# Zero-padding a 64-row matmul to 128 rows, one more weight block kept on chip, and loads and queries moved behind a weight conversion

## The chip, the cores and the metric

The kernel runs on one NeuronCore of a Trainium2 chip. The metric is the device time of one execution in microseconds (us). Nearly all executions of one kernel here agree within 0.3%. A ratio is the mean time of one kernel's fast runs over that of the other kernel's fast runs of the same rounds, so it is not quite the ratio of the medians that stand beside it. "Faster" or "slower" is said for a difference clear of 2%.

Words used throughout: PE is TensorE's matmul pipeline, DVE is VectorE, ACT is ScalarE, POOL is GpSimd, SP is the engine that queues most transfers. In the timelines each of them starts its instructions in the order in which the kernel gives them (weight loads apart), and "in order" below means that. kvd is a unit's k'v as ScalarE copies it out, qT a transposed query, x_n a normalized query, g what follows from h (`maximum(h, 0)**2`), T1 the first difference of w_out's blocks, which product 5 needs. A matmul of 32-bit floats counts as two passes in the timelines (x8 is four matmuls), a transpose as one.

## The reference

```python
# attention without softmax: 8 batches, 8 heads, 576 tokens, head size 64
kv  = einsum('bhsd,bhse->bhde', k, v)                # k'v, contracted over the tokens
out = einsum('bhsd,bhde->bhse', q, kv)
x   = out / sqrt(mean(out*out, -1) + 1e-6) * g_norm  # then reshaped to 4608 x 512
# feed-forward: w_in 512 x 2048, w_out 2048 x 512, both given in 64-bit floats
h = x @ w_in
y = maximum(h, 0)**2 @ w_out
```

576 tokens are four chunks of 128 and a rest of 64. That rest is what the padding is about.

## The kernel before

The feed-forward part runs on nine strips of 512 tokens. Each big product is done by a scheme of seven smaller products on blocks and sums of blocks of the weights (numbers 1 to 7 in the code, taken in the order 1, 2, 6, 5, 7, 3, 4). The first strip's up products use the blocks directly, as the sums are not ready. The weights arrive as 64-bit floats and are turned into 32-bit ones on chip, 32 pieces in 16 pairs, by ScalarE and VectorE. w_out's sums go out to DRAM (`w_out`) and are fetched back block by block in every strip. All this happens while the first strip runs.

```python
def load_rest(b, eng):                       # the last 64 tokens: two batches share 128 partitions
    half = slice(REST * (b % 2), REST * (b % 2 + 1))
    ...
        eng.dma_start(out=rest[n, b // 2][half], in_=src[b, :, C * P : S].rearrange("h s d -> s h d"))

def convert_pieces(ids, dests):
    for i in range(acted[0], min(ids[-1] + 3, len(sources))):
        convert_on_act(i)                    # two ScalarE steps: they wait for the raw piece's load
        acted[0] = i + 1
    # ... four VectorE steps for each of the two pieces ...
    for _ in ids:
        load_piece()                         # next raw piece, into one of four buffers

def sums_out(j):
    t = [wt_pool.tile([P, 5, DH], FP32, name="wt", tag="wt") for _ in js]
    # ... four sums for each of two pieces ...
        nc.sync.dma_start(out=w_out[2:7, :, j, :].rearrange("b p e -> p b e"), in_=x)

def key_value(b, p):                         # one "unit": a batch and a pair of heads
    for c in range(C):
        nc.tensor.matmul(ps, lhsT=flat(tk[:, c]), rhs=tv[:, :, c, :], start=(c == 0), stop=False)
    nc.tensor.matmul(
        ps, lhsT=flat(rest["k", b // 2][half, 2 * p : 2 * p + 2]),      # 64 rows
        rhs=rest["v", b // 2][half, 2 * p : 2 * p + 2], start=False, stop=True,
    )
    # ... ScalarE copies to kvd ...
    if b > 0:
        load_next()                          # the next unit's k, v and q
```

The start, before the first up product:

```python
load_rest(0, nc.gpsimd)
load_piece()
for i in range(3):
    load_piece()
    load_next(nc.gpsimd)
...
for i in range(ready[0]):                    # attention of batch 0, one slice a step
    convert(i // 4 + 1)
    attend(i + 1)
```

## Time and profile before

| | before |
|---|---|
| median, range of the first runs | 1051.1 us, 1050.1 to 1052.0 |
| span of the profiled run, mean granted clock | 1049.1 us, 0.987 |
| PE, DVE, ACT busy | 96%, 40%, 25% |
| DMA moved | 126.6 MB |
| first up product starts | 52.4 us |
| product 6 of strip 0 starts (first to need a block back from DRAM) | 150.5 us |

How to read it: PE is full but for the first 150 us. The lines that show this stand in the prediction, which cuts the run at product 6 of strip 0.

### The profile page before, as it was taken

The page shows a single profiled execution, that of the slowest core. Times are in us where ns is not written, and L with a number is a line of the kernel's source. Part 1 is how long each engine was busy: PE and PEld are TensorE (multiplying, and loading weights), DVE is VectorE, ACT ScalarE, POOL GpSimd, SP SyncE. Part 2 cuts the span into 40 slices and gives each one's busy share as a digit, 9 for nine tenths or more (in the row PEclk, how much of TensorE's full clock was granted, in tenths as well). Part 3 has the DMA queues.
Part 4 walks back from the last instruction along what each step waited for, and adds up shares of the span by engine and source line. Part 5 has one row for each costly group of instructions (what it writes and reads, how often), then busy time and mean ns, then how long its engine had stood idle before and what let it go on. Part 6 is the DMA issues. An engine that isn't in the chain of part 4 may idle for free.

```text
span 1049.1 us, 12212 instructions
## 1 busy us (share of the span) xinstructions
PE 1002.4 (96%) x4864; PEld 855.6 (82%) x4864; DVE 424.3 (40%) x769; ACT 263.4 (25%) x546; POOL 18.4 (2%) x81
## 2 busy tenths in 40 slices
PE   3499799999999999999999999999999999999998
PEld 2444388888888888888888888888888888888887
DVE  2768774335323433333243425322433235413420
ACT  3668420221123211221132103210331122102200
POOL 4000000000000000000000000000000000000000
PEclk9699899999999999999999999999999999999999
DMA  9489965224433344136412650255112330242031
GB/s 239 137 222 303 314 214 178 83 61 128 139 106 85 86 134 147 31 87 189 152 31 61 176 165 26 57 164 186 50 31 91 131 101 1 90 145 87 1 131 70
DMA packets 119210, 126.63 MB, mean 121 GB/s; under 512 B 78225, under 2 KB 102801, under 8 KB 111345
## 3 DMA queue, kind: packets, MB, share of 16 engines
q1 hardware_dynamic: 118464, 124.41, 39.2%
q0 software_dynamic: 528, 1.44, 0.6%
q8 instruction: 38, 0.62, 0.3%
q14 instruction: 20, 0.16, 0.0%
q10 hardware_dynamic: 160, 0.00, 0.0%
HBM read 109.05 MB, written 16.78 MB: 120 GB/s over the span
## 4 chain that ended last, share of the span: by engine, by line
PE 88%; DMA 5%; DVE 3%; ACT 2%; issue 1%; SPq 0%; DVEq 0%; ACTq 0%
PE ps_A L390 45%; PE ps_B L390 22%; PE ps_C L390 11%; PE x_ps L300 2%; DMA raw<-in_moe_w_in_dram 2%; PE kv_ps L268 2%; DMA w_out<-wt 2%; PE xt_ps L327 2%; PE t_ps L253 1%; DMA raw<-in_moe_w_out_dram 1%; PE kv_ps L269 1%; PE ps_A L424 1%; ACT w_c L152 1%; DVE wt L186 1%; ACT raw L155 0%
## 5 line engine op out<-in xcount | busy, mean ns | idle before, releaser
L390 PE MATMUL ps_A<-w_blk,gt 128*128 128x256 f32 x1120 | 249.9, 379 | 0.0
L390 PEld LDWEIGHTS ps_A<-w_blk,gt 128*128 128x128 f32 x1120 | 211.2, 190 | 28.3 <-PE x_ps L295 0.2
L390 PE MATMUL ps_A<-x_t,w_in 128*128 128x256 f32 x768 | 182.4, 380 | 0.6 <-DVE gt L450 0.6
L390 PEld LDWEIGHTS ps_A<-x_t,w_in 128*128 128x128 f32 x768 | 143.8, 190 | 20.4 <-DVE gt L450 1.0
L390 PE MATMUL ps_B<-w_blk,gt 128*128 128x256 f32 x576 | 128.5, 379 | 0.0
L390 PEld LDWEIGHTS ps_B<-w_blk,gt 128*128 128x128 f32 x576 | 108.4, 190 | 14.4 <-issue 0.2
L186 DVE TENSOR_TENSOR gt<-gt 128x512 f32<-128x512 f32 (+1 forms) x54 | 66.2, 1226 | 72.1 <-PE ps_A L390 37.6
L400 ACT COPY snap<-ps_A 128x512 f32<-128x512 f32 x82 | 48.0, 585 | 169.8 <-PE ps_A L390 169.8
L450 DVE TENSOR_TENSOR gt<-ps_C,snap 128x512 f32<-128x512 f32 x32 | 22.1, 691 | 151.6 <-PE ps_C L390 151.6
L451 DVE SCALAR_TENSOR_TENSOR gt<-gt 128x512 f32<-128x512 f32 x96 | 66.4, 692 | 3.3
L450 DVE TENSOR_TENSOR gt<-ps_A,snap 128x512 f32<-128x512 f32 x32 | 22.1, 691 | 109.6 <-PE ps_A L390 109.3
L390 PE MATMUL ps_B<-xT,w_in 128*128 128x256 f32 x256 | 61.1, 382 | 0.0
L390 PE MATMUL ps_A<-xT,w_in 128*128 128x256 f32 x256 | 60.9, 381 | 0.0
L390 PE MATMUL ps_B<-x_t,w_in 128*128 128x256 f32 x256 | 60.5, 379 | 0.0
L390 PE MATMUL ps_C<-xT,w_in 128*128 128x256 f32 x256 | 60.5, 379 | 0.0
L390 PE MATMUL ps_C<-w_blk,gt 128*128 128x256 f32 x256 | 58.1, 381 | 0.0
L305 DVE TENSOR_REDUCE ms<-sq 128x8 f32<-128x512 f32 x36 | 24.6, 684 | 77.8 <-ACT sq L303 77.7
L390 PEld LDWEIGHTS ps_C<-xT,w_in 128*128 128x128 f32 x256 | 48.6, 190 | 6.6
L390 PEld LDWEIGHTS ps_A<-xT,w_in 128*128 128x128 f32 x256 | 48.2, 190 | 6.8
L390 PEld LDWEIGHTS ps_C<-w_blk,gt 128*128 128x128 f32 x256 | 47.7, 190 | 6.6 <-issue 0.2
L390 PEld LDWEIGHTS ps_B<-xT,w_in 128*128 128x128 f32 x256 | 47.6, 190 | 6.7
L390 PEld LDWEIGHTS ps_B<-x_t,w_in 128*128 128x128 f32 x256 | 47.6, 190 | 5.9
(78 smaller groups left out, 853.4 us busy)
## 6 DMA issues: line engine op xcount, KB each, us to landing
w_blk<-w_out SPq DMA_DIRECT2D x61, 1024.0 KB, 5.0
raw<-in_moe_w_in_dram SPq DMA_DIRECT2D x16, 512.0 KB, 5.2
k<-in_k_dram SPq DMA_DIRECT2D x64, 128.0 KB, 3.5
v<-in_v_dram SPq DMA_DIRECT2D x32, 256.0 KB, 3.7
raw<-in_moe_w_out_dram SPq DMA_DIRECT2D x16, 512.0 KB, 5.2
out_dram<-o_sb SPq DMA_DIRECT2D x64, 128.0 KB, 4.8
q<-in_q_dram SPq DMA_DIRECT2D x56, 128.0 KB, 3.5
w_out<-wt SPq DMA_DIRECT2D x8, 640.0 KB, 7.8
```

What stands on the lines that cost most here:

```text
L152: nc.scalar.activation(c, high_f, AF.Abs)
L186: eng.tensor_tensor(out=out, in0=a, in1=b, op=ALU.subtract)
L253: nc.tensor.transpose(ps[:, c, :], flat(t[:, c]), ident)
L268: nc.tensor.matmul(ps, lhsT=flat(tk[:, c]), rhs=tv[:, :, c, :], start=(c == 0), stop=False)
L269: nc.tensor.matmul(ps, lhsT=flat(rest["k", b // 2][half, 2 * p : 2 * p + 2]), rhs=rest["v", b // 2][half, 2 * p : 2 * p + 2], start=False, ...
L300: nc.tensor.matmul(o, lhsT=qT[b, p][:, c_b, :], rhs=kvd[b, p], start=True, stop=True)
L305: nc.vector.reduce_sum(out=ms, in_=by_head(sq), axis=AX.X)
L327: nc.tensor.transpose(ps[:, p, :], t[:, ts(p, P)], ident)
L390: nc.tensor.matmul(bank[BANK[p]][:, i, :], lhsT=lhsT(k), rhs=rhs(k), start=p in (1, 5, 2) and i == 0 and k == 0, stop=k == n - 1, skip_gro ...
L400: nc.scalar.copy(snap[p], b)
L450: nc.vector.tensor_tensor(out=o, in0=b, in1=a, op=ALU.add)
L451: nc.vector.scalar_tensor_tensor(out=o, in0=o, scalar=0.0, in1=o, op0=ALU.max, op1=ALU.mult)
```

## The change

Its intent: take the odd 64-row matmul out of PE's full part, and clear the stretch of the conversion of transfers and of work that can wait. Cut to its core:

```diff
+    k_rest = const.tile([P, H, D], FP32, name="k_rest")
+    v_rest = const.tile([P, 2, H, D], FP32, name="v_rest")     # zero outside batch b % 2's half
...
         nc.tensor.matmul(
-            ps, lhsT=flat(rest["k", b // 2][half, 2 * p : 2 * p + 2]),
-            rhs=rest["v", b // 2][half, 2 * p : 2 * p + 2], start=False, stop=True,
+            ps, lhsT=flat(k_rest[:, 2 * p : 2 * p + 2]), rhs=v_rest[:, b % 2, 2 * p : 2 * p + 2],
+            start=False, stop=True,
         )
...
-        if j + 2 == FQ:                                         # two blocks' stores, early
-            nc.sync.dma_start(out=w_out[0], in_=w_out_11)
-            nc.sync.dma_start(out=w_out[1], in_=w_out_21)
...
-        t = [wt_pool.tile([P, 5, DH], ...
+        t = [wt_pool.tile([P, 4, DH], ...                       # T1 goes to a spare slot of w_in
...
+                for b, t in enumerate(w_first):                 # three blocks' stores, late
+                    nc.sync.dma_start(out=w_out[b], in_=t)
...
-    load_rest(0, nc.gpsimd)
-    load_piece()
-    for i in range(3):
-        load_piece()
+    nc.gpsimd.memset(k_rest, 0.0)
+    nc.gpsimd.memset(v_rest, 0.0)
+    load_next(nc.gpsimd)
+    load_rest(0, nc.gpsimd)
+    for i in range(2):
         load_next(nc.gpsimd)
+        load_piece()
+        load_piece()
...
-        if b > 0:
+        if b < 2:
+            if p == 0:
+                load_next(nc.sync if b else nc.gpsimd)
+        else:
             load_next()
...
     for i in range(ready[0]):
-        convert(i // 4 + 1)
         attend(i + 1)
+        convert((i + 1) // 4)
...
+            if i in (n_up + 6, n_up + 7):                       # batch 2's loads
+                load_next()
+            if i == n_up + 8:
+                load_next()
+                load_rest(2, nc.sync)
...
+            if i < n_up:                                        # batch 1's units, then its queries
+                attend(ready[0] + max(0, (i + 1) - n_up + 2 * NP))
             else:
-                part = (i + 1 - n_up / 2) / (4 + n_up / 2)
-                attend(ready[0] + int((goal - 1 - ready[0]) * min(max(part, 0), 1)) + (part > 1))
+                attend(n_kv + (goal - n_kv) * min(i + 1 - n_up, 6) // 6)
```

The padding leaves the result as it was: `k_rest` holds the 64 rows of both batches of a pair, and the zeros in `v_rest` stand against the other batch's rows.

The parts hang together by memory. The padded `v_rest` takes twice the room of the old one, 4 KB a partition (2 x 8 x 64 x 4 bytes), and beside the old five-block results (4 buffers of 5 KB) the padded kernel did not fit when built alone. Keeping T1 in a slot of `w_in` that is free at that time makes a result 4 KB and so pays for the padding.

More of the change, by code (lines that the diff above doesn't have):

```diff
@@ L86 @@
     ctx.enter_context(tc.manual_schedule())
-    main, rest = {}, {}
+    main = {}
     def load(b, p, q_eng):
@@ L103, in load @@
             main[n, b, p] = t
+    k_rest = const.tile([P, H, D], FP32, name="k_rest")
+    v_rest = const.tile([P, 2, H, D], FP32, name="v_rest")
+    q_rest = {}
     def load_rest(b, eng):
-        half = slice(REST * (b % 2), REST * (b % 2 + 1))
-        for n, src in (("k", k), ("v", v), ("q", q)):
-            if b % 2 == 0:
-                rest[n, b // 2] = rest_pool.tile([P, H, D], FP32, name=f"{n}_rest", tag=f"{n}_rest")
-            eng.dma_start(out=rest[n, b // 2][half], in_=src[b, :, C * P : S].rearrange("h s d -> s h d"))
+        h = b % 2
+        half = slice(REST * h, REST * (h + 1))
+        if h == 0:
+            q_rest[b // 2] = rest_pool.tile([P, H, D], FP32, name="q_rest", tag="q_rest")
+        for t, src in ((k_rest[half], k), (v_rest[half, h], v), (q_rest[b // 2][half], q)):
+            eng.dma_start(out=t, in_=src[b, :, C * P : S].rearrange("h s d -> s h d"))
     units = [(b, p) for b in range(B) for p in range(NP)]
@@ L128 @@
     w_out = dram.tile([7, P, FQ, DH], FP32, name="w_out")
-    w_out_11, w_out_21 = (w_in[:, :, :, b].rearrange("p k g e -> p (k g) e") for b in (4, 5))
+    w_out_11, w_out_21, w_out_t1 = w_first = [
+        w_in[:, :, :, b].rearrange("p k g e -> p (k g) e") for b in (4, 5, 6)
+    ]
     w_in_v = moe_w_in.rearrange("(kc p) (b g f) -> kc g p b f", p=P, b=2, g=NG)
@@ L202, in pieces_out @@
         convert_pieces((NG * NP + j, NG * NP + j + 1), [dest(j), dest(j + 1)])
-        if j + 2 == FQ:
-            nc.sync.dma_start(out=w_out[0], in_=w_out_11)
-            nc.sync.dma_start(out=w_out[1], in_=w_out_21)
     def sums_out(j):
         js = (j, j + 1)
-        t = [wt_pool.tile([P, 5, DH], FP32, name="wt", tag="wt") for _ in js]
+        t = [wt_pool.tile([P, 4, DH], FP32, name="wt", tag="wt") for _ in js]
         convert_pieces([NG * NP + FQ + j for j in js], [x[:, 0:2, :] for x in t])
         for x, j in zip(t, js):
-            minus(nc.vector, x[:, 2], x[:, 0], w_out_11[:, j, :])
-        for x in t:
-            minus(nc.vector, x[:, 3], x[:, 1], x[:, 2])
+            minus(nc.vector, w_out_t1[:, j, :], x[:, 0], w_out_11[:, j, :])
+        for x, j in zip(t, js):
+            minus(nc.vector, x[:, 2], x[:, 1], w_out_t1[:, j, :])
         for x in t:
@@ L217, in sums_out @@
         for x, j in zip(t, js):
-            minus(nc.vector, x[:, 4], w_out_21[:, j, :], x[:, 3])
-            nc.sync.dma_start(out=w_out[2:7, :, j, :].rearrange("b p e -> p b e"), in_=x)
+            minus(nc.vector, x[:, 3], w_out_21[:, j, :], x[:, 2])
+            nc.sync.dma_start(out=w_out[3:7, :, j, :].rearrange("b p e -> p b e"), in_=x)
     conversions = [(pieces_in, i) for i in range(0, NG * NP, 2)]
@@ L229, in convert @@
             converted[0] += 1
+    nc.gpsimd.memset(k_rest, 0.0)
+    nc.gpsimd.memset(v_rest, 0.0)
+    load_next(nc.gpsimd)
     load_rest(0, nc.gpsimd)
-    load_piece()
-    for i in range(3):
+    for i in range(2):
+        load_next(nc.gpsimd)
         load_piece()
-        load_next(nc.gpsimd)
+        load_piece()
     g_col = const.tile([P, 1], FP32, name="g_col")
@@ L256, in transposed_query @@
         if b % 2:
-            t = rest["q", b // 2][:, 2 * p : 2 * p + 2]
+            t = q_rest[b // 2][:, 2 * p : 2 * p + 2]
             ps = apsum.tile([P, P], FP32, name="tr_ps", tag="at")
@@ L264, in key_value @@
         tk, tv = main.pop(("k", b, p)), main.pop(("v", b, p))
-        half = slice(REST * (b % 2), REST * (b % 2 + 1))
         ps = apsum.tile([P, P], FP32, name="kv_ps", tag="at")
@@ L283, in key_value @@
                 load_rest(b + 1, nc.sync)
-        elif p == 0:
-            load_next(nc.gpsimd)
     def query(n):
@@ L377 @@
     A_IN = {1: 0, 2: 2, 3: 6, 4: 3, 5: 4, 6: 5, 7: 1}
-    B_OUT = {1: 0, 2: 1, 3: 3, 4: 6, 5: 4, 6: 5, 7: 2}
+    B_OUT = {1: 0, 2: 1, 5: 2, 7: 3, 3: 4, 6: 5, 4: 6}
     bank, snap, gq, w_blk = {}, {}, {}, {}
@@ L460, in up @@
         combine(p, relu_squared(11), relu_squared(12), last, relu_squared(22))
-    to_stream = iter([(s, p) for s in range(N_STRIP) for p in ORDER][2:])
-    w_blk[0, 1], w_blk[0, 2] = w_out_11, w_out_21
+    w_blk[0, 1], w_blk[0, 2], w_blk[0, 5] = w_first
+    to_stream = iter([(s, p) for s in range(N_STRIP) for p in ORDER if (s, p) not in w_blk])
     def stream():
@@ L479, in down @@
         del w_blk[s, p]
-        if s > 0 or p not in (1, 2):
+        if s > 0 or p not in (1, 2, 5):
             stream()
@@ L529 @@
                     stream()
+                for b, t in enumerate(w_first):
+                    nc.sync.dma_start(out=w_out[b], in_=t)
             fn(*a)
-            if s == 0 and i == n_up:
-                sums_g(quarters(0, NG - 1))
-            if s == 0 and i == n_up + 6:
-                for g in range(NG):
-                    sums_in(g)
             done += w
@@ L538 @@
                 attend(ready[s] + int((goal - ready[s]) * min(done / (0.85 * total), 1)))
-            else:
-                part = (i + 1 - n_up / 2) / (4 + n_up / 2)
-                attend(ready[0] + int((goal - 1 - ready[0]) * min(max(part, 0), 1)) + (part > 1))
+                continue
+            if i == n_up:
+                sums_g(quarters(0, NG - 1))
+            if i in (n_up + 6, n_up + 7):
[3 more added lines that the diff above has]
+                load_rest(2, nc.sync)
+                for g in range(NG):
+                    sums_in(g)
+            n_kv = ready[0] + 2 * NP
+            if i < n_up:
+                attend(ready[0] + max(0, (i + 1) - n_up + 2 * NP))
+            else:
+                attend(n_kv + (goal - n_kv) * min(i + 1 - n_up, 6) // 6)
 _INS = ['q', 'k', 'v', 'g_norm', 'moe_w_in', 'moe_w_out']
```

## The prediction

> **What bounds the kernel now.** I read the page's top and slices first, then windows cut at the events of PE's timeline, then the waits of the stretch in which PE idles, then the chain of waits and the timelines that explain them.
>
> ```profile
> PE   3499799999999999999999999999999999999998
> PEclk9699899999999999999999999999999999999999
> DMA  9489965224433344136412650255112330242031
> ```
>
> A slice is 26 us. Only the first five slices are not full of PE, and there the DMA row is at 9. The windows give it in us (stretch, length, busy of PE, weight load, VectorE, ScalarE, GpSimd, clock, DMA share, GB/s):
>
> ```profile
> 0.00:13.90 13.90, 0.00 (x0) 0.02 (x1) 3.98 (x8) 3.74 (x5) 7.61 (x17) 1.00 0.87 177
> 13.90:30.60 16.70, 12.14 (x56) 10.15 (x56) 6.59 (x15) 8.11 (x18) 4.10 (x18) 0.90 1.07 286
> 30.60:52.40 21.80, 8.84 (x50) 7.63 (x49) 15.76 (x44) 11.96 (x24) 0.00 (x0) 0.68 0.37 119
> 52.40:100.00 47.60, 47.56 (x130) 22.82 (x130) 36.03 (x76) 36.13 (x81) 0.00 (x0) 0.97 0.89 254
> 100.00:132.70 32.70, 22.13 (x86) 12.16 (x87) 25.33 (x62) 17.50 (x47) 1.16 (x8) 0.90 1.08 317
> 132.70:150.50 17.80, 17.80 (x102) 16.05 (x101) 11.14 (x25) 4.40 (x10) 0.60 (x5) 1.00 0.81 276
> 150.50:1049.00 898.50, 893.88 (x4446) 786.79 (x4444) 325.46 (x544) 181.52 (x364) 4.91 (x34) 1.00 0.32 100
> ```
>
> 150.5 us is my checkpoint: there PE begins product 6 of strip 0's second matmul, the first that needs a w_out block which went to DRAM and came back. Behind it PE is full (only the last store, 4.6 us, is idle), so that part, 898.5 us, shrinks only if PE has less to do. Ahead of it are two bounds: a start of 52.4 us, and 100 to 132.7, in which PE idles 10.6 us while DMA is at 1.08. The waits of 60 to 150 us:
>
> ```profile
> ACT w_c L152 <- DMA raw<-in_moe_w_out_dram: 15.6, 5, 5.4
> PE x_ps L295 <- ACT kvd L278: 6.6, 1, 6.6
> SPq L469 <- DMA w_out<-wt: 6.0, 1, 6.0
> ```
>
> PE's longest wait is for kvd, but ScalarE was not slow: in its in-order queue that copy stood behind a conversion step waiting for its raw weight. The chain shows the same queue of transfers:
>
> ```profile
> 105.51 8.76 DMA w_out<-wt
> 115.56 9.09 DMA w_out<-wt
> ...
> 125.50 2.68 DVE wt L186 x8
> ```
>
> So what ends last ahead of the checkpoint is the conversion: its final pair of pieces leaves VectorE at 128.2 us, the last results are queued at 132.9 (behind batch 2's loads in the same queue), and the first blocks are asked back at 141.3.
>
> In the full part the extra work is one form:
>
> ```profile
> 201.49 1.05 PE L268 MATMUL kv_ps<-v,k 128*128 128x128 f32 x8
> 202.47 0.49 PE L269 MATMUL kv_ps<-v_rest,k_rest 64*128 64x128 f32 x2
> 202.89 1.99 PE L390 MATMUL ps_A<-x_t,w_in 128*128 128x256 f32 x8
> 204.72 1.89 PE L390 MATMUL ps_B<-x_t,w_in 128*128 128x256 f32 x8
> ```
>
> Read starts, not durations. Eight 128-row passes take 0.98 us to the next start, the two 64-row passes 0.42, and the eight passes behind them 1.83, where the same eight take 1.73 elsewhere.
>
> **What the Trainium skill says.** "TensorEngine Tiling (Array Packing)", Key Properties: changing the tiling mode drains TensorE, changing only the tile does not. The trace agrees: the passes on either side of the 64-row form are late. "TensorE: Matmul & The Clock Gate", LDWEIGHTS: the load's time follows the columns, not the rows contracted. Padding to 128 rows should then cost nothing; the trace has one column count only (186 ns for 64 rows, 192 for 128), which fits. Same page, Part 1: an idle window brings PE's clock down to half. The trace shows 0.68 in 30.6 to 52.4 us, and the first up product after a wait takes 5.3 us where later ones take 3.4. "DMA: Bandwidth & Descriptors", Anatomy of one DMA: a transfer completes only when its last write is acknowledged, and HBM is the slowest target. Agrees: w_out pieces land in a median 7.8 us, raw weights, of similar size, in 5.2.
>
> **The change, part by part.**
>
> *Padded v.* Per unit (batch and head pair) the cost now is 0.98 + 0.42 + 0.10 (delay of the passes behind) = 1.50 us. Ten passes at the 0.11 us of a full 128-column pass (eight x_ps passes take 0.89) are 1.10. It saves 0.40. Of 32 units, batches 2 to 7, 24 units, lie in the full part: 24 x 0.40 = 9.6 us, all on the path. The 8 others lie where PE waits anyway: counted as nothing. Added are two GpSimd memsets of 512 and 1024 columns; scaled from 0.22 us for 128 columns, an estimate of 2 to 3 us ahead of the first q load. They shift it, but q now goes ahead of the rests in that queue, so I take it as even. The other row-tiling user (the rest queries, a 64-column form) is left as it is.
>
> *T1 on chip.* The same VectorE operations, one writing into w_in's spare slot. The results shrink from 640 to 512 KB a piece: 8 x 128 KB = 1 MB less in the bound stretch. Two 1 MB copies to DRAM (queued at 94 and 95 us) become three behind the first block requests: 2 MB leave the stretch. One block of 61 need not be fetched.
>
> *Loads moved.* Three units of batch 2 (3 x 768 KB) and its rest (384 KB), 2.7 MB, leave the stretch, and with them their waits in the issue queue. Together 5.7 MB less; at that window's 317 GB/s this is 18 us of DMA time. What then limits? One pair of conversion costs VectorE 3.7 us, and the last four also 2.7 us of sums: 6.4. From 93.4 us (pair 13 of 16 begins) four pairs and two g sums (2 x 1.3) take 28 us without waits: 121 us, where it took until 128.2. Pair 13 itself I leave near its place: the pairs before it come at 5.4 us each ((93.4 - 50.3)/8), set by the loop buffer free, load 5.2 us, ScalarE 1.2 us, with four buffers, which nothing in the change shortens. Then the last result is queued at once: 121 us, lands in 6 (8 before, less traffic) 127, the block comes back in some 6: 133.
>
> *Queries moved.* They no longer stand before product 1. ScalarE finishes the last raw pieces at about 112 and the activations that product 1 needs at 114; products 1 and 2 are 4 x 3.46 = 13.8 us, and the slices put between them (three full queries of 0.89, one rest query of some 2, two transposes of 0.44) 5.6: PE is at product 6 at 133. Both sides thus meet at about 133.5. One query and one transpose fewer lie ahead of the checkpoint than before (three full, not four; two transposes, not three): 1.3 us are still to do.
>
> *The start.* Attention's loads come before the weights and ScalarE's copies before the raw steps, so the wait at 24.8 us (qT behind raw) goes, and one conversion goes behind the fourth query. I estimate the first up product at 47 instead of 52.4. But conversion then begins later (first pair at some 17 us instead of 10.7), and the pair that is fifth starts at about 49, against 50.3. As the conversion sets the checkpoint, I count nearly nothing of these 5 us.
>
> Sum: the checkpoint comes at 133.5 instead of 150.5 (-17.0), the left-over work +1.3, k'v -9.6: -25.3. 1051.1 - 25.3 = 1025.8, so 1026.
>
> **The rivals.**
>
> *A: k'v alone counts (the round trip through DRAM takes the place of the wait).* All w_out writes must land before product 6. For it: SP's wait of 6.0 us for w_out, and the 9 us writes in the chain. If block 6 comes only at 140, PE idles 6 or 7 us at product 6: 1032. Against it: the queue is nearly empty behind the last pair.
>
> *B: what was moved collides later.* Behind the checkpoint there are now three 1 MB stores, batch 2's loads, and the sums over w_in, which move from product 5 to product 7 as they overwrite the slots that the stores read. They take VectorE 10.9 us (157.4 to 168.1 now), and product 7's combination stands behind them, with product 4's bank behind that. I see about 6.9 us of slack (product 3). If the stores are late, 2 to 5 us are given back: 1028 to 1031. For it: w_out's two copies took 8.1 us to land. Against: DMA share is only 0.47 in 150 to 190 us.
>
> *C: the start counts in full.* If the loop of raw buffers has slack, the earlier up products and relus carry through, and the checkpoint comes at 128 to 129: 1021. For it: ScalarE waited for PE twice (3.1 and 1.3 us) in the loop. Against: the 5.4 us a pair.
>
> *D: padded k'v costs as much as before* (the drain is due to something else, such as v's other read pattern): 1035. Against: the passes of 128 rows just before it use the same kind of operands and are not late.
>
> **Range and chances.** 2% is at 1030.1. A alone or D alone ends above it, B on its border, C well below. I give A in strength 0.12, B 0.15, D 0.04, C 0.25. Range 1018 to 1036. Faster by over 2%: 0.72; within 2%: 0.27; slower 0.01, as nothing is added to the full part.
>
> **What would show it.** k'v units: from the start of their eight passes to the end of the eight up passes behind, 2.83 instead of 3.23 us. Product 6's first matmul at 133.5. Conversion's last VectorE sum at 121, with DMA share below 1 from 100 to 120. First up product near 47. No PE wait of over 1 us in products 7, 3, 4 of strip 0 or in strip 1. I am wrong if PE idles for block 6, if the fifth pair starts well after 50 us (the start then costs the conversion), or if PE shows gaps between 135 and 200 us.

## The result, and the profile after

The changed kernel takes 1031.9 us (median; 1031.4 to 1033.3) against 1051.5 in the same rounds: ratio 0.9818, 95% interval 0.9801 to 0.9835. Unaltered, it was run a second time among the last experiments: 1031.9, ratio 0.9812. So it gains 19.6 us, 1.8%, just short of the 2% line (the second interval, 0.9791 to 0.9833, reaches over it), and the time is 6 us above the predicted 1026.

The page's slices after the change (tenths of busy PE, granted clock and DMA in 40 equal slices):

```profile
PE   3599999999999999999999999999999999999998
PEclk9699999999999999999999999999999999999999
DMA  9389797134422433244413640274012420251032
```

PE's gap in the fifth slice (7 before) is gone; the start is hardly better. The windows, cut at the first up product, at product 1 and at product 6 (columns as in the prediction):

```profile
0.00:49.50 49.50, 20.61 (x104) 18.36 (x104) 22.25 (x58) 21.55 (x43) 12.82 (x37) 0.81 0.68 178
49.50:119.30 69.80, 66.12 (x188) 32.34 (x189) 57.08 (x125) 54.41 (x125) 0.00 (x0) 0.94 0.85 255
119.30:138.70 19.40, 18.97 (x115) 16.55 (x113) 16.29 (x38) 5.08 (x13) 1.17 (x8) 1.00 0.69 240
138.70:1029.70 891.00, 886.33 (x4462) 784.95 (x4460) 328.26 (x551) 183.01 (x367) 5.55 (x38) 1.00 0.34 106
```

Product 6 comes at 138.7 instead of 150.5, and what follows takes 891.0 us instead of 898.6. So -11.8 and -7.6 make the 19.4 us by which the span shrank.

The shorter remainder is the padding. PE's timeline around one unit, to compare with the four lines in the prediction:

```profile
191.42 1.05 PE L276 MATMUL kv_ps<-v,k 128*128 128x128 f32 x8
192.31 0.39 PE L277 MATMUL kv_ps<-v_rest,k_rest 128*128 128x128 f32 x2
192.54 1.89 PE L399 MATMUL ps_A<-x_t,w_in 128*128 128x256 f32 x8
194.27 1.89 PE L399 MATMUL ps_B<-x_t,w_in 128*128 128x256 f32 x8
```

From first pass to the end of the eight passes behind, 2.85 us instead of 3.23. The two padded passes take 0.23 us to the next start, as other 128-row passes do (0.11 each), and the passes behind them are no longer late.

The earlier product 6 is the stretch in which PE waited. PE's timeline there (a bracket is a wait and what ended it):

```profile
104.36 0.33 PE L268 MATMUL tr_ps<-ident,q_rest 128*128 128x128 f32 x1 [2.18 <-ACT qT L264]
104.53 5.29 PE L433 MATMUL ps_B<-xT,w_in 128*128 128x512 f32 x8
...
119.31 3.62 PE L399 MATMUL ps_A<-w_in,gt 128*128 128x256 f32 x16
...
128.92 0.65 PE L336 MATMUL xt_ps<-ident,x_n 128*128 128x128 f32 x4 [0.43 <-DVE x_n L325]
...
138.70 1.68 PE L399 MATMUL ps_A<-w_blk,gt 128*128 128x256 f32 x7
```

The long wait for kvd is gone, and PE does not wait for block 6 at 138.7. Three waits remain that the prediction did not have. At 93 and 104 us PE waits 1.5 and 2.2 us for copies that ScalarE makes late, and the up product behind the second wait takes 5.1 us to the next start instead of 3.4 (granted clock there 0.67). At 128.9 it waits for the normalized first query of batch 1 from VectorE. That wait is short here, but in the second profiled run of the same kernel product 1 began earlier, at 116.8, and PE waited 2.47 us at the same place; product 6 came at 138.2 all the same:

```profile
116.76 3.62 PE L399 MATMUL ps_A<-w_in,gt 128*128 128x256 f32 x16
...
128.41 0.66 PE L336 MATMUL xt_ps<-ident,x_n 128*128 128x128 f32 x4 [2.47 <-DVE x_n L325]
...
138.19 2.11 PE L399 MATMUL ps_A<-w_blk,gt 128*128 128x256 f32 x9
```

So the transpose at 128.9 holds product 6, though in the first profiled run PE's own pace came within 0.4 us of being the bound itself. VectorE's timeline says why the transpose is late:

```profile
122.78 0.75 DVE L195 TENSOR_TENSOR wt<-w_in,wt 128x256 f32<-128x256 f32 x2
123.46 0.68 DVE L424 TENSOR_TENSOR gt<-gt 128x512 f32<-128x512 f32 x1
...
126.11 0.68 DVE L314 TENSOR_REDUCE ms<-sq 128x8 f32<-128x512 f32 x1
...
128.18 0.69 DVE L325 TENSOR_TENSOR x_n<-x_ps,rms 128x512 f32<-128x512 f32 x1
```

The conversion's last sums end at 123.5, two pairs of sums over g follow, and only then the query's turn comes, though PE was done with it at 123.9. The conversion still rules the start, by another door.

### The profile page after: what moved, and what is told of

Its sections match the earlier page's. It is cut to its first block, busy times and chain, and to the rows that moved or that the text cites. A ratio compares the mean times of both kernels' runs of the same rounds, so it can differ in the third digit from the quotient of the medians.

```text
span 1029.7 us, 12226 instructions
## 1 busy us (share of the span) xinstructions
PE 992.0 (96%) x4864; PEld 852.2 (83%) x4864; DVE 423.9 (41%) x769; ACT 264.0 (26%) x546; POOL 19.5 (2%) x83
## 4 chain that ended last, share of the span: by engine, by line
PE 87%; DVE 4%; DMA 4%; ACT 3%; SPq 1%; issue 1%; DVEq 0%; ACTq 0%
PE ps_A L399 45%; PE ps_B L399 23%; PE ps_C L399 11%; PE x_ps L309 3%; DMA raw<-in_moe_w_in_dram 2%; PE kv_ps L276 2%; PE xt_ps L336 2%; DMA raw<-in_moe_w_out_dram 2%; PE t_ps L262 1%; ACT w_c L161 1%; DVE wt L195 1%; SPq L97 1%; ACT raw L164 1%; DVE w_c L185 1%; PE kv_ps L277 1%
## 5 line engine op out<-in xcount | busy, mean ns | idle before, releaser
L399 PE MATMUL ps_B<-w_blk,gt 128*128 128x256 f32 x544 | 121.5, 379 | 0.0
L399 PEld LDWEIGHTS ps_B<-w_blk,gt 128*128 128x128 f32 x544 | 102.4, 190 | 13.6 <-issue 0.2
L459 DVE TENSOR_TENSOR gt<-ps_A,snap 128x512 f32<-128x512 f32 x32 | 22.1, 691 | 108.4 <-PE ps_A L399 108.1
L399 PEld LDWEIGHTS ps_B<-x_t,w_in 128*128 128x128 f32 x256 | 47.6, 190 | 5.9
L399 PEld LDWEIGHTS ps_B<-xT,w_in 128*128 128x128 f32 x256 | 47.6, 190 | 5.9
```

The costliest lines, as they stand in the source:

```text
L399: nc.tensor.matmul(bank[BANK[p]][:, i, :], lhsT=lhsT(k), rhs=rhs(k), start=p in (1, 5, 2) and i == 0 and k == 0, stop=k == n - 1, skip_gro ...
L459: nc.vector.tensor_tensor(out=o, in0=b, in1=a, op=ALU.add)
```

## The experiments

Twelve kernels ran, in three sessions on one chip each. All gave right results except the one that was wrong. The table shows all of them with the before and the after; the times inside the run are from each kernel's profiled execution. "Sums end" is the end of VectorE's last w_out sum. "Rest" is from product 6 to the end of the span.

| run | median us | ratio to before | first up | sums end | product 1 | product 6 | rest |
|---|---|---|---|---|---|---|---|
| before | 1051.5 | 1 | 52.4 | 128.2 | 132.7 | 150.5 | 898.6 |
| after | 1031.9 | 0.9818 | 49.5 | 123.5 | 119.3 | 138.7 | 891.0 |
| x12 after again | 1031.9 | 0.9812 | 49.7 | 123.0 | 116.8 | 138.2 | 891.0 |
| x1 padding and T1 alone | 1038.2 | 0.9873 | 51.6 | 121.5 | 126.0 | 145.5 | 889.3 |
| x2 no padding | 1040.0 | 0.9894 | 49.2 | 122.9 | 119.1 | 138.1 | 900.3 |
| x3 old start | 1030.0 | 0.9790 | 52.1 | 120.9 | 115.2 | 137.6 | 891.0 |
| x4 stores early | 1034.6 | 0.9835 | 49.9 | 126.0 | 121.5 | 141.1 | 891.1 |
| x5 loads early | 1030.4 | 0.9790 | 49.6 | 121.9 | 115.2 | 137.2 | 891.2 |
| x6 queries early | 1036.6 | 0.9854 | 48.9 | 122.6 | 127.2 | 145.0 | 889.3 |
| x7 raw ahead | 1023.9 | 0.9733 | 47.6 | 111.4 | 110.9 | 129.5 | 891.1 |
| x8 rest twice (on before) | 1057.1 | 1.0050 | 54.4 | 130.6 | 135.2 | 153.0 | 903.8 |
| x9 raw ahead, third pair late | 1020.4 | 0.9702 | 45.0 | 109.4 | 108.4 | 126.9 | 891.1 |
| x10 third pair late | 1033.8 | 0.9828 | 45.7 | 124.8 | 118.3 | 141.3 | 891.1 |
| x11 raw ahead, old start | 1027.2 | 0.9765 | 52.4 | 116.3 | 115.8 | 134.4 | 891.0 |

The last column is the table's first lesson. With padding the rest is 891.0 to 891.2 us, or 889.3 in x1 and x6, where one query and two transposes (1.7 us) are already done ahead of product 6. Without padding it is 900.3 (x2) and 898.6 (before, with those queries done). So the time splits cleanly in two, and every experiment but x2 and x8 is about when product 6 starts.

**x2: the padding undone.** The matmul again takes 64 rows; all else is the changed kernel.

```diff
-            ps, lhsT=flat(k_rest[:, 2 * p : 2 * p + 2]), rhs=v_rest[:, b % 2, 2 * p : 2 * p + 2],
+            ps, lhsT=flat(k_rest[half, 2 * p : 2 * p + 2]), rhs=v_rest[half, b % 2, 2 * p : 2 * p + 2],
```

> The changed kernel with the last k'v pass taken over 64 rows again, all else kept (zeroes included). Theory 1 (switching to the 64-row form and back costs 0.385 us a unit, and 24 units lie where PE is full): the time rises by 9.3 us to 1041, and the interval from a unit's first pass to the end of the eight up passes behind it is 3.23 us again. Rival (the padding is worth nothing, the gain is all from loads and stores): 1032.

1040.0 us. The rest grew by 9.3 us (900.3 - 891.0), as expected; product 6 came 0.6 earlier, hence 8.7 in span (8.1 in the medians). PE did not wait at the transpose there: this run was bound by PE's own pace. The padding is nearly half of the gain.

**x8: why 64 rows cost more.** The kernel before with the 64-row matmul done twice. Its output is wrong, which doesn't matter for the time.

```diff
+        for again in range(2):
             nc.tensor.matmul(
                 ps, lhsT=flat(rest["k", b // 2][half, 2 * p : 2 * p + 2]),
-                rhs=rest["v", b // 2][half, 2 * p : 2 * p + 2], start=False, stop=True,
+                rhs=rest["v", b // 2][half, 2 * p : 2 * p + 2], start=False, stop=again == 1,
```

> The kernel before with the 64-row pass of k'v done twice (a wrong result on purpose). If the cost is a drain at the change of form, the second matmul (two passes) adds 0.22 us a unit, 24 x 0.22 = 5.3 us: 1056.5. If 64-row passes are slow themselves (0.21 us each), it adds 0.42 a unit, 10 us: 1061.5. The starts in PE's timeline tell it directly.

1057.1 us: a rest of 903.8 instead of 898.6, 5.2 more. PE's timeline of one unit:

```profile
203.91 1.05 PE L268 MATMUL kv_ps<-v,k 128*128 128x128 f32 x8
204.90 0.71 PE L270 MATMUL kv_ps<-v_rest,k_rest 64*128 64x128 f32 x4
205.53 1.99 PE L391 MATMUL ps_A<-x_t,w_in 128*128 128x256 f32 x8
207.37 1.89 PE L391 MATMUL ps_B<-x_t,w_in 128*128 128x256 f32 x8
```

Four 64-row passes take 0.63 us where two took 0.42. The second matmul adds 0.21, the price of two ordinary passes. So the 64-row passes are not slow; going into that form and out of it costs about 0.4 us once, with four passes in it as with two.

**x1: padding and T1 without the rest of the change.** The kernel before with `v_rest`, four-block results, T1 in `w_in`'s slot and the three late stores; its old order of loads, start and queries. Cut to its core, on the kernel before:

```diff
-            ps, lhsT=flat(rest["k", b // 2][half, 2 * p : 2 * p + 2]),
-            rhs=rest["v", b // 2][half, 2 * p : 2 * p + 2], start=False, stop=True,
+            ps, lhsT=flat(k_rest[:, 2 * p : 2 * p + 2]), rhs=v_rest[:, b % 2, 2 * p : 2 * p + 2],
+            start=False, stop=True,
...
-        if j + 2 == FQ:
-            nc.sync.dma_start(out=w_out[0], in_=w_out_11)
-            nc.sync.dma_start(out=w_out[1], in_=w_out_21)
...
-        t = [wt_pool.tile([P, 5, DH], FP32, name="wt", tag="wt") for _ in js]
+        t = [wt_pool.tile([P, 4, DH], FP32, name="wt", tag="wt") for _ in js]
...
+                for b, t in enumerate(w_first):
+                    nc.sync.dma_start(out=w_out[b], in_=t)
```

> The kernel before with padded v and T1 on chip (three stores behind the first block requests), but its old order of loads, start and queries. Theory 1: 9.3 us from k'v, and product 6 of strip 0 starts only some 3 to 4 us earlier (147), as batch 2's loads and the queries ahead of product 1 still stand in the way: 1038. Rival A (the stores and T1 were the whole of the early gain): product 6 at 139, 1031. Rival B (they bring nothing): 1042.

1038.2 us, as theory 1 had it, but with product 6 at 145.5, not 147 (the queries done ahead make up the difference). The conversion ends 6.7 us earlier than before (121.5 against 128.2), even though batch 2's loads still run in that stretch. So the relief of the conversion does not need the loads moved, which x5 tests by itself.

**x3, x5: the old start, and batch 2's loads early.**

```diff
 # x3, on the changed kernel
-    load_next(nc.gpsimd)
     load_rest(0, nc.gpsimd)
-    for i in range(2):
-        load_next(nc.gpsimd)
-        load_piece()
-        load_piece()
+    load_piece()
+    for i in range(3):
+        load_piece()
+        load_next(nc.gpsimd)
...
-        attend(i + 1)
-        convert((i + 1) // 4)
+        convert(i // 4 + 1)
+        attend(i + 1)
 # x5, on the changed kernel
-        if b < 2:
-            if p == 0:
-                load_next(nc.sync if b else nc.gpsimd)
-        else:
-            load_next()
-            if p == NP - 1 and b + 1 < B: ...
+        if b > 0:
+            load_next()
+            if p == NP - 1 and b + 1 < B: ...
+        elif p == 0:
+            load_next(nc.gpsimd)
...
-            if i in (n_up + 6, n_up + 7):
-                load_next()
             if i == n_up + 8:
-                load_next()
-                load_rest(2, nc.sync)
```

> The changed kernel with the old start (rests and weights first, conversion ahead of attention in each step). Theory 1 (product 6 is set by PE's work from the first up product on and nearly as much by the conversion): the first up product moves from 49.5 to about 52.4, the conversion's last pair ends 1 to 2 us earlier, product 6 starts 1 to 3 us later: 1033 to 1035. Rival (conversion alone sets it): 1030 to 1032, the same or faster. Rival (the start counts in full as in my rival C): 1037.

> The changed kernel with batch 2's loads (2.7 MB) issued again as batch 1's k'v passes free their buffers, ahead of the last w_out results in the queue. Theory 1: the issue queue holds back raw pieces and results, the last results are queued at about 128 instead of 124, the blocks come back near 140, product 6 starts 3 to 5 us later: 1035 to 1037. Rival (only traffic counts and there is room): 1032 to 1033.

Both misses of my theory, on the side of a rival. x3: 1030.0 us, as the rival that conversion alone sets product 6 had it. The first up product is 2.6 us later, the sums end 2.6 us earlier, and product 6 comes 1.1 us earlier. The transpose comes the full 2.6 us earlier; the rest is lost to the product behind its wait, which takes 5.0 us instead of 3.5:

```profile
126.29 0.81 PE L335 MATMUL xt_ps<-ident,x_n 128*128 128x128 f32 x4 [1.90 <-DVE x_n L324]
126.90 5.18 PE L398 MATMUL ps_C<-w_in,gt 128*128 128x256 f32 x16
131.92 1.05 PE L308 MATMUL x_ps<-kvd,qT 128*128 128x128 f32 x8
```

x5: 1030.4, below even the rival's 1032 to 1033; the last blocks were asked back at 129.7 instead of 128.9, yet nothing waited for them. Their ratios, both 0.9790, touch the interval of the changed kernel, so I do not call them faster. But two of the change's parts, the new start and the later loads, gained nothing.

**x4: the stores early, T1 fetched back.**

```diff
+        if j + 2 == FQ:
+            for b in range(2):
+                nc.sync.dma_start(out=w_out[b], in_=w_first[b])
...
             nc.sync.dma_start(out=w_out[3:7, :, j, :].rearrange("b p e -> p b e"), in_=x)
+            nc.sync.dma_start(out=w_out[2, :, j, :], in_=w_out_t1[:, j, :])
...                                                              # and no late stores
```

> The changed kernel with the three blocks' stores back in the conversion stretch (two after the w_out pieces, T1 with each of the last results) and T1 fetched from DRAM for product 5. It adds 3 MB to that stretch. Theory 1: the last raw pieces come 2 to 4 us later, product 6 starts 2 to 5 us later: 1034 to 1037. Rival (the stores cost nothing while DMA has room): 1032.

1034.6 us. The sums end at 126.0 instead of 123.5 and product 6 comes 2.4 us later, the lower end of what was expected. 3 MB of stores in that stretch do cost, unlike x5's 2.7 MB of loads. What makes the difference was not tried. The traces show where it arises: right behind the two 1 MB stores, queued at 95 us, SP needs 5.4 us for the next two k loads (4.9 in the kernel before, 1.2 in the changed kernel and in x5, with no such stores ahead of them), so the next raw pieces are queued at 105.0 instead of 100.2 (98.1 in x5). In x4, 3.0 of the 5.4 us are put down to a wait for PE; in the kernel before, none are.

**x6: batch 1's queries early again.** The old formula for spreading attention over the first strip, in the changed kernel:

```diff
-            n_kv = ready[0] + 2 * NP
-            if i < n_up:
-                attend(ready[0] + max(0, (i + 1) - n_up + 2 * NP))
-            else:
-                attend(n_kv + (goal - n_kv) * min(i + 1 - n_up, 6) // 6)
+            part = (i + 1 - n_up / 2) / (4 + n_up / 2)
+            attend(ready[0] + int((goal - 1 - ready[0]) * min(max(part, 0), 1)) + (part > 1))
```

> The changed kernel with batch 1's units and queries spread as before over the second half of the up products and the first five steps behind them. Theory 1: PE meets the rest query ahead of the last up product, in order behind kvd copies that ScalarE does only after the last raw pieces (about 115), so product 1 starts at about 123 instead of 119.3, but with one or two queries done: product 6 2 to 4 us later: 1034 to 1036. Rival (the queries' place does not matter, as PE has the same work to do by product 6): 1032.

1036.6 us, just above the expected range: product 1 came at 127.2, not at about 123, held by VectorE and not by the kvd copies that I had named. PE's timeline:

```profile
102.71 0.48 PE L268 MATMUL tr_ps<-ident,q_rest 128*128 128x128 f32 x1 [3.87 <-ACT qT L264]
...
126.71 0.66 PE L336 MATMUL xt_ps<-ident,x_n 128*128 128x128 f32 x4 [2.31 <-DVE x_n L325]
127.20 3.62 PE L399 MATMUL ps_A<-w_in,gt 128*128 128x256 f32 x16
```

The first transposed query waits for VectorE until 126.7, much as in the changed kernel (128.9). But in the changed kernel product 1 comes ahead of this transpose, here behind it: moving the queries lets PE do product 1 while the conversion ends. It is worth 4.6 us of span (product 6 at 145.0, less the 1.7 of work done ahead).

**x7: raw pieces further ahead.** The prediction held that four raw buffers set the conversion's pace. A raw piece and a four-block result are both 4 KB a partition, so one pool of eight can serve both, at the same memory, and six pieces can be on the way.

```diff
-    raw_pool = conv.enter_context(tc.tile_pool(name="raw", bufs=4))
-    wt_pool = conv.enter_context(tc.tile_pool(name="wt", bufs=4))
+    raw_pool = conv.enter_context(tc.tile_pool(name="raw", bufs=8))
...
         for _ in ids:
-            load_piece()
+            if len(raw) < 28 or ids[-1] >= 25:
+                load_piece()
...
+            raw_pool.tile([P, 2, WN // 2], I64, name="wt", tag="raw").bitcast(FP32)
...
         attend(i + 1)
+        if i == 1:
+            load_piece()
+            load_piece()
```

> The changed kernel with raw pieces and w_out results sharing one pool of eight buffers of the same size, so that six raw pieces are on the way instead of four until the last four pairs. Theory 1 (the conversion goes at 5.4 us a pair because each load waits for a buffer, and ScalarE's copies wait behind it, which holds PE up by 3.7 us and cools it): pairs go at about 4 us, the last one ends near 112, PE no longer waits for qT, product 1 starts at about 113.5 instead of 119.3, product 6 at 133: 1026. Rival (DMA bandwidth, not buffers, sets the pace): pairs at 5.4 us as before, 1032.

1023.9 us, ratio 0.9733: faster than before, and 2 us better than expected; the first up product also came earlier (47.6). The waits of 60 to 150 us, first the changed kernel, then x7:

```profile
ACT w_c L161 <- DMA raw<-in_moe_w_out_dram: 8.4, 8, 4.0
PE tr_ps L268 <- ACT qT L264: 3.7, 2, 2.2
```

```profile
ACT w_c L160 <- DMA raw<-in_moe_w_out_dram: 1.4, 2, 0.9
```

The conversion's pairs, from the fifth to the thirteenth, come at 4.3 us each instead of 5.5, the sums end at 111.4 instead of 123.5, and PE does not wait once between the first up product and product 6:

```profile
47.60:110.90 63.30, 63.30 (x189) 31.57 (x190) 60.01 (x134) 53.74 (x125) 0.00 (x0) 0.97 0.85 256
110.90:129.40 18.50, 18.50 (x114) 16.40 (x113) 12.68 (x29) 5.03 (x13) 1.16 (x8) 1.00 0.85 300
```

**x9, x10, x11: two edits, each with and without raw ahead.** If the conversion rules the changed kernel and PE rules x7, the same edit must have two different effects. One edit moves the third conversion pair behind the fourth query's normalization. The other is x3's old start.

```diff
 # x9 on x7, x10 on the changed kernel
-        convert((i + 1) // 4)
+        convert((0, 0, 0, 1, 1, 1, 1, 2, 2, 2, 2, 2, 2, 2, 2, 4)[i])
 # x11 is x7 with x3's edit
```

> The kernel with raw pieces loaded ahead, and the third conversion pair moved behind the fourth query's normalization (it stood between the third and the fourth on VectorE). Theory 2 (once the conversion has slack, PE is busy from the first up product on, so what the start gains counts in full): first up product 3.7 us earlier (about 43.9), no new waits, product 6 at about 125.7, 3.7 us faster than with raw ahead alone: 1020. Rival (the conversion still sets product 6): the same as with raw ahead alone, 1024.

> The changed kernel, without raw ahead, with that same move of the third pair. Theory 2 (in the changed kernel the conversion's end on VectorE sets the first rest query's normalization, and through it product 6): first up product 3.7 us earlier, but the raw loop of four buffers starts 2 to 4 us later, so product 6 comes 2 to 3 us later: 1033 to 1035. Rival (PE's start sets it): 3.7 us faster, 1028.

> The kernel with raw pieces ahead, with the old start. Theory 2: what cost nothing in the changed kernel (old start: 1030) costs in full here, as PE is the bound: first up product at 51 to 52 instead of 47.6, about 4 us slower than raw ahead alone: 1028. Rival (the conversion still sets it): 1022 to 1024.

> The changed kernel itself, unaltered, in the same rounds as the others, as a measure of how much sessions differ: 1030 to 1033, ratio to before 0.980 to 0.983.

| edit | on the changed kernel: first up, product 6 | on x7: first up, product 6 |
|---|---|---|
| third pair late | -3.9, +2.6 us (x10) | -2.6, -2.5 us (x9) |
| old start | +2.6, -1.1 us (x3) | +4.8, +4.9 us (x11) |

On x7 product 6 moves by what the first up product moves. On the changed kernel it moves the other way, with the end of the sums (+1.3 in x10, -2.6 in x3), and in both the product behind the wait runs slower as well (x3 above), which takes 1.1 us from x10 and keeps x3 from gaining more. The medians have the same signs: on the changed kernel +1.9 (x10) and -1.9 us (x3), on x7 -3.5 (x9) and +3.4 (x11). PE's timeline of x10:

```profile
130.16 1.11 PE L336 MATMUL xt_ps<-ident,x_n 128*128 128x128 f32 x4 [2.72 <-DVE x_n L325]
131.07 4.75 PE L399 MATMUL ps_C<-w_in,gt 128*128 128x256 f32 x16
```

The matmul behind the wait of 2.72 us, part of product 2, takes 4.6 us to the next start instead of 3.5, and the granted clock from there to product 6 is 0.86, not 1.00. The opposite signs in the table settle which one is the bound: the conversion in the changed kernel, PE in x7. x9, at 1020.4 us and a ratio of 0.9702, beats the kernel before by 3% and the changed one by 1.1%. x12, the changed kernel again without an edit, came out as expected, so the sessions can be compared.

## Why the prediction was right or wrong

The time fell inside the range (1018 to 1036), but 6 us above the point, and on the other side of the 2% line than the one I had given 0.72. By its steps:

- **Padded v: right.** Predicted 0.40 us a unit and 9.6 us; measured 0.39 and 9.3 (x2, and before against x1: 898.6 - 889.3). x8 shows a price paid once per change of form, as a drain would have it; the drain itself no trace shows. x2 reads the same tiles over 64 rows and is slow again, so rival D is out.
- **Left-over work: small.** Predicted 1.3 us; it is 1.7, as four transposes, not three, stood ahead of product 6 before.
- **"The checkpoint comes at 133.5 instead of 150.5 (-17.0)": the term that was mis-sized.** It measured -11.8, and this is nearly the whole error. The step had two sides that "meet at about 133.5". Both came 5 us late (VectorE's part at 126.1 instead of 121, product 6 at 138.7), for connected reasons.
  - *"four pairs and two g sums (2 x 1.3) take 28 us without waits: 121 us".* VectorE began that part at 94.9, not 93.4, waited 1.4 us for ScalarE's step on a raw piece, and had three g sums to do before the query's turn, not two. It was done at 126.1 (the last w_out sum at 123.5).
  - *The conversion was tied to product 6 by the wrong wait.* I tied it through the block's way to DRAM and back (rival A's wait). The blocks were asked for at 128.9, some 10 us ahead of need, and PE never waited for them. What ties it is the first rest query's normalization, behind the conversion in VectorE's order. From that transpose at 128.9, PE's own work to product 6 is 9.8 us.
  - *"activations that product 1 needs at 114".* ScalarE was 1 us late (115.0), but PE was not there: the first up product came at 49.5, not 47, and PE lost 3.7 us waiting for copies behind ScalarE's raw steps and 1.7 to the slow up product behind the second of these waits. That alone mattered little, as x12 shows with product 1 at 116.8 and the same product 6.
- **"Loads moved": no gain shown.** I counted their 2.7 MB and "their waits in the issue queue" into the 18 us of relief. x5 puts them back and is not slower. What freed the stretch was T1 and the stores (x1; x4 gives 2.4 us for undoing the stores alone) and, for product 6, the queries' place (x6, 4.6 us).
- **"I count nearly nothing of these 5 us" for the start: right that nothing was gained, but one of its terms was wrong.** The fifth pair was to start "at about 49, against 50.3". It started at 51.2 (50.0 with the old start, x3), so the sign "the start then costs the conversion" came true in part: 2.6 us at the sums' end, by x3. The reason given, four buffers that set the pair's pace, is shown by x7: with six pieces on the way, the sums end 12 us earlier.
- **Rivals B and C.** B did not happen: PE shows no wait in strip 0 behind product 6. C, "if the loop of raw buffers has slack ... the checkpoint comes at 128 to 129", describes x7 (129.5), not this kernel.
- **Readings of lines.** PE is full in the third and fourth slice, and the DMA row of the first five reads 9, 4, 8, 9, 9, not 9 throughout; nothing rests on it. The 5.3 us of a slow up product is a duration; by starts it is 5.1 against 3.4. The slow landing of w_out's pieces is weaker support for the page than "agrees" says: they were 640 KB against 512, the section cited is about transfers that GpSimd queues, and these are queued by SP. In the changed kernel, with 512 KB both, the pieces landed in a median 4.5 us and the raw weights in 5.4. The output's 128 KB stores are better support: 4.8 us in the kernel before, against 3.5 for k's 128 KB loads.

Together: -11.8 + 1.7 - 9.3 = -19.4, the fall of the span. What stays open is why the loads behind two 1 MB stores are queued so slowly, and with them why 3 MB of stores delay the conversion when 2.7 MB of loads do not; and when a wait of 2 us is followed by a slow product.

## What to carry to other kernels

Look for a full engine's lone odd-shaped instruction and price the change of form around it, by the next starts, not by its duration: here 64 rows padded with zeros to 128 were cheaper than 64. When a stretch ahead of the full part is a race of several chains, list for every in-order engine what stands behind the slow chain, as the chain you relieve may hold the end through another wait than the one you saw. And before more work is moved out of such a stretch, test with one experiment which chain is the bound: the same edit of the start cost 5 us or gained 1 at product 6, depending on whether six or four pieces were on the way.

## What the Trainium skill lacked or had wrong

- "TensorEngine Tiling (Array Packing)", Key Properties, says that changing the tiling mode drains TensorE, but not what it costs. Here one excursion to a 64-row form and back cost 0.39 us beside 128-row work (24 units, 9.3 us). A second matmul inside it added only 0.21 us.
- The same page recommends row tiling where the contracted size is at most 64 and has no word on a lone small matmul among full ones. There zero-padding was cheaper: 0.23 us for the two padded passes, against 0.42 with delays of 0.09 ahead of them and 0.10 behind.
- "TensorE: Matmul & The Clock Gate", Part 1, ties the loss of clock to an idle window of about 3.4 us. Here shorter waits sufficed at times: behind waits of 2.2 (changed kernel), 1.9 (x12, x3) and 2.7 us (x10) a product took 5.1, 5.1, 5.0 and 4.6 us instead of 3.4 to 3.5. Behind others as long, 2.0 (kernel before), 2.5 (x12) and 2.7 us (x10, at 83 us), it took 3.4 to 3.5. What decides is not shown here.
- No page has a figure for how in-order ScalarE work behind a load wait shows up elsewhere; here 8.4 us of such waits (w_out's pieces, 60 to 150 us) stood beside 3.7 us of PE waits for unrelated copies, and with two more pieces on the way 1.4 us and none were left.
